# First mixture of a three-stage kernel: second product in whole float32 from an unsplit w2, and the low parts of w1 all on VectorE

## The chip, the cores and the metric

The program runs on one core of a Trainium2 chip. TensorE (PE in the profile) multiplies, VectorE (DVE), ScalarE (ACT) and GpSimd (POOL) do elementwise work, and SyncE (SP) and GpSimd issue the DMAs. The metric is the device time of one execution in microseconds.

## The reference

```
x   = attention(q, k, v)                       # 4 x 8 heads x 576 x 64 -> 2304 tokens of 512
# first mixture: 8 experts, 288 tokens each, given out greedily by logit
logits = x @ w_gate
...
for e in range(8):
    mask = assigned == e                       # 288 tokens
    h = np.maximum(x[mask] @ w1[e], 0.0)       # w1[e]: 512 x 1024
    out[mask] = h @ w2[e]                      # w2[e]: 1024 x 512
# second mixture: two of 8 experts for each token, weighted
logits = x @ w_gate2 + log1p(exp(x @ w_noise)) * noise
...
    out[mask] += top2_w[mask, k, None] * (np.maximum(x[mask] @ w1[e], 0.0) @ w2[e])
```

All tensors are float32.

## The kernel before

There are three stages. Attention fills the first 190 us or so, the first mixture runs from about 220 to 578 us, and the second mixture from there to the end.

In both mixtures a product is made of float32r operands. A float32 array is split in a high part, a rounded copy in float32r (written by ScalarE), and a low part, the array minus the copy (written by VectorE or GpSimd). Each product is three matmuls, in the order of `TERMS`: high by high, high by low, low by high.

An expert n of the first mixture (0 to 7) goes through these steps:

- `route()` finds the tokens of the next expert by counting digits of the logits. A digit is a loop between VectorE and TensorE: VectorE compares (`A`, L624), TensorE counts (`psR`, L633), VectorE tests (`F`, L635), TensorE adds up (L639), VectorE forms the next digit (`vv`, L642). All tiles of this loop but the counts are in SBUF.
- `compact()` makes the token list and gathers the rows of x by three indirect DMAs from GpSimd's queue (`xg`, L728). `xprep1()` transposes them on TensorE (L819) and splits them.
- `weights()` loads w1 and w2 into the four buffers `raw` and splits each in four pieces of 128 x 1024. ScalarE writes the high part (L745); the low part (L747) goes to VectorE or GpSimd by the lists D0 to D4. For experts 0 to 3 VectorE takes two low parts of w1 and GpSimd the other two of w1 and all four of w2. For experts 4 to 7 VectorE takes all four of w1 and two of w2, and GpSimd the other two of w2.
- `gemm_a()` makes the first product (`gemm1`, L835: 8 blocks of 12 matmuls with 288 columns), `relu` writes its result as a high part hh (ScalarE, L847) and a low part hl (VectorE, L848), and the second product (L876) makes 4 blocks of 24 matmuls with 288 columns.
- `rows()` transposes the result, stores it, multiplies it by the gate weights of the second mixture (L910), and `gate2()` works out that mixture's routing in pieces.

`weave` sets the order. Each of these is a generator that yields an estimated time, and the next instructions come from the generator with the smallest clock. Every engine then works through its own list strictly in that order, so a TensorE instruction of the routing that waits for VectorE holds up the products behind it.

Of the kernel before, what the change touches and what calls it, by code (L numbers as in the profile page):

```python
# [536 lines left out]
def moe(ctx, tc, g):  # L537
# [40 lines left out]
    # big buffers  # L578
# [3 lines left out]
    hh = mp.tile([P, KF, SL], F32R, name="hh")  # L582
    hl = mp.tile([P, KF, SL], F32R, name="hl")
    w1 = [[mp.tile([P, FF], F32R, name=f"w1{j}{i}") for i in range(KD)] for j in range(2)]
    w2 = [[mp.tile([P, 2, DM], F32R, name=f"w2{j}{i}") for i in range(KF // 2)] for j in range(2)]
# [8 lines left out]
    # ---- routing of the first mixture  # L594
# [102 lines left out]
    def compact():  # L697
        oh = T["oh"]
        for ph in range(E):
# [3 lines left out]
            # token numbers of the group  # L703
# [30 lines left out]
    # ---- operands of the products, split in two float32r parts  # L734
# [21 lines left out]

    def load2(n, i):
        if n < E:
            src = g["w2a"][bass.ds(REG[n], 1), 2 * i * P:2 * (i + 1) * P, :].rearrange("e (a p) d -> p (e a) d", p=P)
        else:  # L760
            src = g["w2b"][n - E, 2 * i * P:2 * (i + 1) * P, :].rearrange("(a p) d -> p a d", p=P)
        raw_load((2, n, i), src)
# [3 lines left out]
    DV = 4  # L766
    D1 = (1, 3)
    D2 = ()
    D3 = (0, 1, 2, 3)
    D4 = (1, 3)  # L770
    D5 = (3,)
    D6 = (1, 3)
    D0 = (1, 3)

    def on_dve(m, n, i):
        if n >= E:
            return i in (D5, D6)[m - 1]
        if n >= DV:
            return i in (D3, D4)[m - 1]
        return i in (D0 if n == 0 and m == 1 else (D1, D2)[m - 1])  # L780

    def weights():
        for n in range(2 * E):
# [5 lines left out]
            if n < E:  # L789
                yield 6.0  # L790
            yield lambda n=n: emitted["g1"] >= n - 1
            for i in range(KD):
                split((1, n, i), w1[0][i], w1[1][i], on_dve(1, n, i))
                load2(n, i)
                yield 2.4
            emitted["w1"] = n
            yield lambda n=n: emitted["g2"] >= n - 1
            for i in range(KD):
# [28 lines left out]
    HH = (hh, hl)  # L827
# [18 lines left out]
    def relu(pg, f, cols):  # L846
        nc.scalar.activation(hh[:, f, cols], pg, AF.Relu)  # L847
        RELU[0] = nc.vector.scalar_tensor_tensor(hl[:, f, cols], pg, 0.0, hh[:, f, cols].bitcast(F32), op0=OP.max,  # L848
                                                 op1=OP.subtract)

# [4 lines left out]
    def gemm_a():  # L855
        for n in range(E):
# [3 lines left out]
            for f in range(KF):  # L860
                x = gemm1(cols, f)
                if pend:
                    relu(*pend)
# [3 lines left out]
            relu(*pend)  # L867
# [3 lines left out]
            for d in range(KD):  # L871
                pg = ps.tile([P, 512], F32, name="psG", bufs=3)
                k_ = 0
                for f in range(KF):
                    for a, b in TERMS:
                        nc.tensor.matmul(pg[:, :CAP], w2[a][f // 2][:, f % 2, d * P:(d + 1) * P], HH[b][:, f, cols],  # L876
                                         start=k_ == 0, stop=k_ == 3 * KF - 1)
                        k_ += 1
                    if f % 2:
                        yield 6 * CAP / 2400  # L880
# [43 lines left out]
    def slots(a, c0, c1):  # L924
        """source row, row of out and weight of slots, from their digits"""
# [148 lines left out]
    # experts with more than SLOT tokens: a list of the further tiles, worked through at the end  # L1074
# [40 lines left out]
    # ---- the second mixture  # L1115
# [234 lines left out]
```

## Time and profile before

| | us |
|---|---|
| Median of 3 runs | 1051.91 (1051.02 to 1058.09) |
| Profiled execution: first to last instruction (its span, the only time kept of it) | 1046.5 |
| Median less that span | 5.4 |
| First mixture: start of the first product of expert 0 to the last second product | 220 to 578.4 |
| TensorE busy in that stretch | 294.9 of 358.4 |
| GpSimd busy in that stretch | 124.4 |

The profile comes from one execution. Durations are read from it, and a forecast for the runs adds the 5.4 us that lie outside of the span.

### The profile page before, as it was taken

What the parts mean: (1) busy time and instruction counts of PE and PEld (TensorE: products, weight loads), DVE (VectorE), ACT (ScalarE), POOL (GpSimd) and SP (SyncE); (2) the same over time, 40 slices, a digit from 0 to 9 for tenths busy, and PEclk for the clock granted to TensorE, in tenths of its full rate; (3) what the DMA queues carried; (4) which work ended last, traced back from release to release, by engine and by line L of the source; (5) the groups of instructions that cost most, each with busy time, mean ns of one, the idle gap of its engine ahead of it and who ended that gap; (6) DMA issues with size and microseconds to landing.
All of it is one profiled execution on the core that took longest, in us unless ns stands there. A gap on an engine that the chain in (4) does not pass through costs nothing. (4 is left out here: it accounts for less than half of the span.)

```text
span 1046.5 us, 18783 instructions
## 1 busy us (share of the span) xinstructions
PE 935.8 (89%) x6798; PEld 864.0 (83%) x6798; DVE 671.3 (64%) x1804; ACT 402.3 (38%) x807; POOL 556.4 (53%) x636
## 2 busy tenths in 40 slices
PE   7999999558786869969987898999999999999996
PEld 6999999457776869959986877989898988899895
DVE  8776777586777888866776747373747465646521
ACT  6767776043232423442634304422322333333310
POOL 9424332162324241330254768797878888878712
PEclk9999999668887879989998999999999999999999
DMA  9868732055242343444443425253534444442301
GB/s 198 190 136 185 174 97 73 22 185 185 56 147 65 109 145 109 126 135 153 148 160 111 142 71 179 88 178 121 170 125 163 133 144 154 130 165 89 124 27 51
DMA packets 115568, 135.15 MB, mean 129 GB/s; under 512 B 68856, under 2 KB 78072, under 8 KB 115472
## 3 DMA queue, kind: packets, MB, share of 16 engines
q1 hardware_dynamic: 98384, 90.93, 30.4%
q0 software_dynamic: 17088, 42.98, 13.3%
q8 instruction: 55, 0.90, 0.4%
q14 instruction: 41, 0.34, 0.1%
HBM read 110.91 MB, written 24.53 MB: 129 GB/s over the span
## 5 line engine op out<-in xcount | busy, mean ns | idle before, releaser
L835 PE MATMUL psG<-xh,w 128*128 128x312 f32 (+3 forms) x1536 | 351.1, 316 | 12.7 <-DVE y L1265 5.9
L835 PEld LDWEIGHTS psG<-xh,w 128*128 128x128 f32 x1536 | 267.2, 198 | 16.7 <-DVE y L1265 7.4
L747 POOL TENSOR_TENSOR w<-raw,w 128x1024 fp32r<-128x1024 f32 x72 | 181.9, 2549 | 155.2 <-ACT w L745 123.5
L835 PE MATMUL psG<-xl,w 128*128 128x312 f32 (+3 forms) x768 | 241.2, 314 | 0.3 <-DVE tot L1106 0.3
L1233 PE MATMUL psG<-w,hh 128*128 128x512 f32 (+1 forms) x640 | 199.9, 390 | 0.0
L1127 POOL DMA_INDIRECT xrow<-x_dram,sr x160 | 156.7, 980 | 53.6 <-issue 45.3
L848 DVE SCALAR_TENSOR_TENSOR hl<-psG,hh 128x312 fp32r<-128x312 f32 (+3 forms) x192 | 89.5, 470 | 143.4 <-ACT hh L847 143.4
L847 ACT ACTIVATE hh<-psG 128x312 fp32r<-128x312 f32 (+3 forms) x192 | 80.9, 423 | 261.0 <-PE psG L835 259.0
L745 ACT ACTIVATE w<-raw 128x1024 fp32r<-128x1024 f32 x128 | 131.8, 1055 | 62.2 <-PE psG L1233 27.1
L835 PEld LDWEIGHTS psG<-xl,w 128*128 128x128 f32 x768 | 151.9, 198 | 0.9 <-DVE tot L1106 0.5
L1233 PEld LDWEIGHTS psG<-w,hh 128*128 128x128 f32 (+1 forms) x640 | 118.4, 185 | 26.7
L747 DVE TENSOR_TENSOR w<-raw,w 128x1024 fp32r<-128x1024 f32 x56 | 116.8, 2089 | 19.0 <-ACT w L745 18.7
L1233 PE MATMUL psG<-w,hl 128*128 128x512 f32 (+1 forms) x320 | 125.0, 391 | 0.0
L876 PE MATMUL psG<-hh,w 128*128 128x288 f32 x512 | 121.3, 318 | 0.0
L876 PEld LDWEIGHTS psG<-hh,w 128*128 128x128 f32 x512 | 90.8, 202 | 11.4 <-issue 11.2
L876 PE MATMUL psG<-hl,w 128*128 128x288 f32 x256 | 81.0, 316 | 6.6 <-DVE hl L848 6.6
L327 POOL DMA_DIRECT2D xq<-x_dram x60 | 33.0, 556 | 93.8 <-DMA x_dram<-xr 33.0
L728 POOL DMA_INDIRECT xg<-x_dram,ix x24 | 26.0, 1085 | 89.6 <-DVE w L422 72.6
L1267 POOL DMA_INDIRECT out_dram<-y,sx x40 | 43.6, 1089 | 53.3 <-DVE y L1265 45.4
L1233 PEld LDWEIGHTS psG<-w,hl 128*128 128x128 f32 (+1 forms) x320 | 59.3, 185 | 12.7
L1151 ACT ACTIVATE xh<-xt 128x512 fp32r<-128x512 f32 (+1 forms) x40 | 23.1, 617 | 113.4 <-DVE xt L1147 113.4
L253 PE MATMUL pO<-v,pt 128*128 128x65 f32 x448 | 58.9, 269 | 0.2
(282 smaller groups left out, 1460.5 us busy)
## 6 DMA issues: line engine op xcount, KB each, us to landing
raw<-in_moe_w_dram SPq DMA_DIRECT2D x128, 512.0 KB, 3.9
x_dram<-xr SPq DMA_DIRECT2D x18, 264.0 KB, 2.1
out_dram<-zero POOLq DMA_DIRECT2D x18, 256.0 KB, 3.5
x_dram<-x2r SPq DMA_DIRECT2D x96, 48.0 KB, 2.4
rawk<-in_k_dram SPq DMA_DIRECT2D x16, 256.0 KB
rawq<-in_q_dram SPq DMA_DIRECT2D x16, 256.0 KB, 4.5
v<-in_v_dram SPq DMA_DIRECT2D x16, 256.0 KB, 5.3
xq<-x_dram POOLq DMA_DIRECT2D x60, 64.0 KB, 3.5
```

Source lines behind the costliest of these rows:

```text
L253: nc.tensor.matmul(o[:, hh + s, :], pt[:, s, j, :], (vp, vc)[j][:, 2 * hp + s, :], start=j == js[0], stop=j == 1)
L327: (nc.gpsimd if XQP else nc.sync).dma_start(xq[32 * a:32 * (a + 1)], x_dram[c * P:(c + 1) * P, a * P:(a + 1) * P].rearrange("(u t) c -> t ...
L728: nc.gpsimd.indirect_dma_start(out=xg[t], out_offset=None, in_=x_dram[:, :], in_offset=bass.IndirectOffsetOnAxis(ap=ix[:, t:t + 1], axis=0))
L745: nc.scalar.activation(h, t, AF.Copy)
L747: eng.tensor_tensor(l, t, h.bitcast(F32), op=OP.subtract)
L835: nc.tensor.matmul(pg[:, :n], w1[a][kd][:, f * P:(f + 1) * P], XX[b][:, kd, cols], start=k_ == 0, stop=k_ == 3 * KD - 1)
L847: nc.scalar.activation(hh[:, f, cols], pg, AF.Relu)
L848: RELU[0] = nc.vector.scalar_tensor_tensor(hl[:, f, cols], pg, 0.0, hh[:, f, cols].bitcast(F32), op0=OP.max, op1=OP.subtract)
L876: nc.tensor.matmul(pg[:, :CAP], w2[a][f // 2][:, f % 2, d * P:(d + 1) * P], HH[b][:, f, cols], start=k_ == 0, stop=k_ == 3 * KF - 1)
L1127: nc.gpsimd.indirect_dma_start(out=t[:, u * P:(u + 1) * P], out_offset=None, in_=src, in_offset=bass.IndirectOffsetOnAxis(ap=SRC[e, j][u], ...
L1233: nc.tensor.matmul(py[:m], HH[b][:, f, j * P:j * P + m], w2[a][f // 2][:, f % 2, :], start=k_ == 0, stop=k_ == 3 * KF - 1)
L1267: x = nc.gpsimd.indirect_dma_start(out=out[:, :], out_offset=bass.IndirectOffsetOnAxis(ap=IDX[e, j][:n], axis=0), in_=y, in_offset=None, b ...
```

## The change

For the first mixture only:

- w2 is loaded whole, as float32, straight into the tiles that hold the split parts of w2 in the second mixture (`w2f`, two sets of four, one for even and one for odd experts). It is no longer split: 32 high parts on ScalarE and 32 low parts go.
- The first product's result is written once, as float32 (`hf`, two buffers, one for even and one for odd experts), by ScalarE. The 64 low parts hl on VectorE go.
- The second product is one matmul in whole float32 where it was three in float32r: 32 for an expert instead of 96.
- All four low parts of w1 are on VectorE for every expert. The number of these pieces on VectorE stays at 32 in the first mixture, and on GpSimd goes from 32 to none.
- The load of w2 for expert n is issued as soon as the second product of expert n - 2 stands in the program, in one row behind the load of w1. Before, each of its four pieces stood behind a split of w1.
- `weave` is told 8 x 288 / 2400 us instead of 6 x 288 / 2400 us for two matmul groups of the second product.

```diff
+    hf = [mp.tile([P, KF, SL], F32, tag=f"h{j}", name=f"hf{j}", bufs=1)[:, :, :CAP] for j in range(2)]
...
     def load2(n, i):
         if n < E:
             src = g["w2a"][bass.ds(REG[n], 1), 2 * i * P:2 * (i + 1) * P, :].rearrange("e (a p) d -> p (e a) d", p=P)
-        else:
-            src = g["w2b"][n - E, 2 * i * P:2 * (i + 1) * P, :].rearrange("(a p) d -> p a d", p=P)
+            t = W2F[n, i] = mp.tile([P, 2, DM], F32, tag=f"w2{n % 2}{i}", name="w2f", bufs=1)
+            nc.sync.dma_start(t, src)
+            return
+        src = g["w2b"][n - E, 2 * i * P:2 * (i + 1) * P, :].rearrange("(a p) d -> p a d", p=P)
         raw_load((2, n, i), src)
...
     def on_dve(m, n, i):
-        if n >= E:
-            return i in (D5, D6)[m - 1]
-        if n >= DV:
-            return i in (D3, D4)[m - 1]
-        return i in (D0 if n == 0 and m == 1 else (D1, D2)[m - 1])
+        return n < E or i in (D5, D6)[m - 1]
...
             if n < E:
                 yield 6.0
+                yield lambda n=n: emitted["g2"] >= n - 2
+                for i in range(KD):
+                    load2(n, i)
             yield lambda n=n: emitted["g1"] >= n - 1
             for i in range(KD):
                 split((1, n, i), w1[0][i], w1[1][i], on_dve(1, n, i))
-                load2(n, i)
+                if n >= E:
+                    load2(n, i)
                 yield 2.4
             emitted["w1"] = n
+            if n < E:
+                emitted["w2"] = n
+                continue
...
+    def relu_whole(n, pg, f, cols):
+        nc.scalar.activation(hf[n % 2][:, f, :], pg, AF.Relu)
...
                 for f in range(KF):
-                    for a, b in TERMS:
-                        nc.tensor.matmul(pg[:, :CAP], w2[a][f // 2][:, f % 2, d * P:(d + 1) * P], HH[b][:, f, cols],
-                                         start=k_ == 0, stop=k_ == 3 * KF - 1)
-                        k_ += 1
+                    nc.tensor.matmul(pg[:, :CAP], W2F[n, f // 2][:, f % 2, d * P:(d + 1) * P], hf[n % 2][:, f, :],
+                                     start=f == 0, stop=f == KF - 1)
                     if f % 2:
-                        yield 6 * CAP / 2400
+                        yield 8 * CAP / 2400
```

GpSimd's list before, from the gathers of expert 0 to those of expert 2 (`w` are parts of w1 and w2):

```order
L728 DMA xg<-x_dram,ix 96x528 x3
L747 TENSOR_TENSOR w_3095<-raw,w_3091 128x1024
L747 TENSOR_TENSOR w_3097<-raw,w_3093 128x1024
L747 TENSOR_TENSOR w_3103<-raw,w_3099 128x1024
L747 TENSOR_TENSOR w_3104<-raw,w_3100 128x1024
L747 TENSOR_TENSOR w_3105<-raw,w_3101 128x1024
L747 TENSOR_TENSOR w_3106<-raw,w_3102 128x1024
L728 DMA xg<-x_dram,ix 96x528 x3
```

And GpSimd's list now, from there to the first weights of the second mixture (`xrow` are gathers of that mixture):

```order
L1278 MEMSET spacer 1x1 x39
L737 DMA xg<-x_dram,ix 96x528 x24
L1139 DMA xrow<-x_dram,sr_6852 128x128 x12
L756 TENSOR_TENSOR w_3093<-raw,w_3089 128x1024
L756 TENSOR_TENSOR w_3094<-raw,w_3090 128x1024
L756 TENSOR_TENSOR w_3095<-raw,w_3091 128x1024
```

The 24 gathers of the eight experts stand in one row, with no elementwise work between them.

VectorE's list before, where w1 of expert 1 is split while the next expert is routed:

```order
L624 TENSOR_TENSOR A<-vv,jrow 128x9x32
L629 SCALAR_TENSOR_TENSOR u<-vv,dg 128x18
L848 SCALAR_TENSOR_TENSOR hl<-psG,hh 128x288
L747 TENSOR_TENSOR w_3096<-raw,w_3092 128x1024
L635 TENSOR_SCALAR F<-psR 16x8
L642 TENSOR_SCALAR vv<-u,psR 128x18
L624 TENSOR_TENSOR A<-vv,jrow 128x2304
L629 SCALAR_TENSOR_TENSOR u<-vv,dg 128x18
L747 TENSOR_TENSOR w_3098<-raw,w_3094 128x1024
L635 TENSOR_SCALAR F<-psR 128x8
```

And VectorE's list now at the same place (L633, L638, L644, L651 and L756 are L624, L629, L635, L642 and L747 of before):

```order
L633 TENSOR_TENSOR A<-vv,jrow 128x9x32
L638 SCALAR_TENSOR_TENSOR u<-vv,dg 128x18
L756 TENSOR_TENSOR w_3093<-raw,w_3089 128x1024
L644 TENSOR_SCALAR F<-psR 16x8
L756 TENSOR_TENSOR w_3094<-raw,w_3090 128x1024
L651 TENSOR_SCALAR vv<-u,psR 128x18
L633 TENSOR_TENSOR A<-vv,jrow 128x2304
L638 SCALAR_TENSOR_TENSOR u<-vv,dg 128x18
L756 TENSOR_TENSOR w_3095<-raw,w_3091 128x1024
L644 TENSOR_SCALAR F<-psR 128x8
L818 TENSOR_TENSOR xl<-psT,xh 128x288 x2
L651 TENSOR_SCALAR vv<-u,psR 128x18
```

The low part hl is gone from the routing loop, and two more low parts of w1 stand in it.

## Rows read from the trace of the kernel before

**Rows 1.** The page, its head and part 1: busy us, share, instructions.

```profile
span 1046.5 us, 18783 instructions
PE 935.8 (89%) x6798; PEld 864.0 (83%) x6798; DVE 671.3 (64%) x1804; ACT 402.3 (38%) x807; POOL 556.4 (53%) x636
```

**Rows 2.** Windows: stretch, length, busy us by engine, granted clock (PEclk), DMA.

```profile
220.00:578.40 358.40, 294.93 (x2545) 281.59 (x2546) 266.40 (x789) 132.16 (x238) 124.41 (x69) 0.87 0.41 126
...
503.80:532.90 29.10, 29.07 (x231) 28.26 (x229) 25.05 (x80) 16.17 (x27) 6.50 (x3) 1.00 0.52 166
...
605.00:1046.50 441.50, 422.39 (x2400) 378.46 (x2398) 227.96 (x269) 126.53 (x212) 322.58 (x284) 1.00 0.38 125
```

**Rows 3.** Waits of TensorE, 215 to 580 us: total, times, longest.

```profile
PE psR L633 <- DVE A L624: 15.8, 3, 8.5
PE psT L819 <- DMA xg<-x_dram,ix: 10.9, 5, 4.4
PE psQ L1010 <- DVE gM L997: 7.6, 1, 7.6
PE psR L676 <- DVE sc L673: 6.9, 1, 6.9
PE psG L876 <- DVE hl L848: 6.6, 3, 2.8
PE psQ L1053 <- DVE gmd L1051: 6.0, 3, 3.6
PE psR L639 <- DVE F L635: 3.4, 1, 3.4
```

**Rows 4.** Timeline, 318 to 335 us, three engines: start, duration, instruction [idle before].

```profile
322.95 9.28 POOL L747 TENSOR_TENSOR w<-raw,w 128x1024 fp32r<-128x1024 f32 x4
...
322.42 9.85 DVE L642 TENSOR_SCALAR vv<-u,psR 128x18 bf16<-128x18 f32 x1 [0.71 <-PE psR L639]
332.30 1.36 DVE L624 TENSOR_TENSOR A<-vv,jrow 128x2304 bf16<-128x2304 bf16 x1
...
333.72 0.64 PE L633 MATMUL psR<-O,A 128*128 128x8 bf16 x18 [8.50 <-DVE A L624]
```

**Rows 5.** Groups of instructions, 190 to 600 us: low parts of weights.

```profile
L747 POOL TENSOR_TENSOR w<-raw,w 128x1024 fp32r<-128x1024 f32 x37 | 94.7, 2582 | 153.3 <-ACT w L745 122.0 <-PE psG L876 30.9 <-PE psG L835 0.3
...
L747 DVE TENSOR_TENSOR w<-raw,w 128x1024 fp32r<-128x1024 f32 x35 | 46.7, 1342 | 1.3 <-ACT w L745 1.0 <-issue 0.2
```

**Rows 6.** Matmuls of attention in whole float32: durations min/median/max in ns; timeline.

```profile
L188 PE MATMUL pS<-kf,qf x64: 275/275/579, 7.0 to 146.5; 128*128 128x128 f32 x64
...
L253 PE MATMUL pO<-v,pt x448: 218/275/325, 15.7 to 181.3; 128*128 128x65 f32 x150
...
94.63 0.61 PE L188 MATMUL pS<-kf,qf 128*128 128x128 f32 x4
```

**Rows 7.** Timeline, second product of expert 0 in float32r.

```profile
262.72 0.29 PE L876 MATMUL psG<-hl,w 128*128 128x288 f32 x1
...
263.51 0.29 PE L876 MATMUL psG<-hl,w 128*128 128x288 f32 x1
```

**Rows 8.** Windows of the 15 stretches at half clock: TensorE, granted clock.

```profile
329.30:343.00 13.70, 9.28 (x70) 0.51 0.25 52
...
sum 92.80, PE 74.49; mean PE 4.97
```

**Rows 9.** Timeline of VectorE, 405 to 416 us: low parts of w1 of expert 4.

```profile
408.61 1.22 DVE L747 TENSOR_TENSOR w<-raw,w 128x1024 fp32r<-128x1024 f32 x1
...
414.42 1.22 DVE L747 TENSOR_TENSOR w<-raw,w 128x1024 fp32r<-128x1024 f32 x1
```

**Rows 10.** Gathers of x: two on GpSimd's timeline, and their landing time.

```profile
319.56 0.91 POOL L728 DMA_INDIRECT xg<-x_dram,ix  x1 [12.41 <-DVE w L422]
...
450.07 2.81 POOL L728 DMA_INDIRECT xg<-x_dram,ix  x1 [0.30 <-issue]
...
DMA to landing us min/median/max: 3.0/4.6/7.5
```

More of the change, by code (lines that the diff above doesn't have):

```diff
@@ L581, in moe, with second_operands, second_weights @@
     xl = mp.tile([P, KD, SL], F32R, name="xl")
-    hh = mp.tile([P, KF, SL], F32R, name="hh")
-    hl = mp.tile([P, KF, SL], F32R, name="hl")
     w1 = [[mp.tile([P, FF], F32R, name=f"w1{j}{i}") for i in range(KD)] for j in range(2)]
-    w2 = [[mp.tile([P, 2, DM], F32R, name=f"w2{j}{i}") for i in range(KF // 2)] for j in range(2)]
+    hf = [mp.tile([P, KF, SL], F32, tag=f"h{j}", name=f"hf{j}", bufs=1)[:, :, :CAP] for j in range(2)]
+    HH, w2 = [], []
+    def second_operands():
+        if not HH:
+            HH.extend(mp.tile([P, KF, SL], F32R, tag=f"h{j}", name=f"h{'hl'[j]}", bufs=1) for j in range(2))
+    def second_weights():
+        if not w2:
+            w2.extend([mp.tile([P, 2, DM], F32R, tag=f"w2{j}{i}", name=f"w2{j}{i}", bufs=1) for i in range(KF // 2)]
+                      for j in range(2))
     def gpart(n):
@@ L755, in load1 @@
         raw_load((1, n, i), src)
+    W2F = {}
     def load2(n, i):
@@ L759, in load2 @@
             src = g["w2a"][bass.ds(REG[n], 1), 2 * i * P:2 * (i + 1) * P, :].rearrange("e (a p) d -> p (e a) d", p=P)
-        else:
-            src = g["w2b"][n - E, 2 * i * P:2 * (i + 1) * P, :].rearrange("(a p) d -> p a d", p=P)
+            t = W2F[n, i] = mp.tile([P, 2, DM], F32, tag=f"w2{n % 2}{i}", name="w2f", bufs=1)
+            nc.sync.dma_start(t, src)
+            return
+        src = g["w2b"][n - E, 2 * i * P:2 * (i + 1) * P, :].rearrange("(a p) d -> p a d", p=P)
         raw_load((2, n, i), src)
     REG = {}
[L766 to L770, printed above, removed]
     D5 = (3,)
     D6 = (1, 3)
-    D0 = (1, 3)
     def on_dve(m, n, i):
-        if n >= E:
-            return i in (D5, D6)[m - 1]
-        if n >= DV:
-            return i in (D3, D4)[m - 1]
-        return i in (D0 if n == 0 and m == 1 else (D1, D2)[m - 1])
+        return n < E or i in (D5, D6)[m - 1]
     def weights():
@@ L793, in weights @@
                 split((1, n, i), w1[0][i], w1[1][i], on_dve(1, n, i))
-                load2(n, i)
+                if n >= E:
+                    load2(n, i)
                 yield 2.4
             emitted["w1"] = n
+            if n < E:
+                emitted["w2"] = n
+                continue
             yield lambda n=n: emitted["g2"] >= n - 1
+            second_weights()
             for i in range(KD):
@@ L826, in moe @@
     XX = (xh, xl)
-    HH = (hh, hl)
     def gemm1(cols, f):
@@ L846, in relu @@
     def relu(pg, f, cols):
+        second_operands()
+        hh, hl = HH
         nc.scalar.activation(hh[:, f, cols], pg, AF.Relu)
@@ L862, in gemm_a @@
                 if pend:
-                    relu(*pend)
+                    relu_whole(n, *pend)
                 pend = x
@@ L866, in gemm_a @@
             emitted["g1"] = n
-            relu(*pend)
+            relu_whole(n, *pend)
             yield lambda n=n: emitted["w2"] >= n
@@ L872, in gemm_a @@
                 pg = ps.tile([P, 512], F32, name="psG", bufs=3)
-                k_ = 0
                 for f in range(KF):
-                    for a, b in TERMS:
-                        nc.tensor.matmul(pg[:, :CAP], w2[a][f // 2][:, f % 2, d * P:(d + 1) * P], HH[b][:, f, cols],
-                                         start=k_ == 0, stop=k_ == 3 * KF - 1)
-                        k_ += 1
+                    nc.tensor.matmul(pg[:, :CAP], W2F[n, f // 2][:, f % 2, d * P:(d + 1) * P], hf[n % 2][:, f, :],
+                                     start=f == 0, stop=f == KF - 1)
                     if f % 2:
-                        yield 6 * CAP / 2400
+                        yield 8 * CAP / 2400
                 if pend:
```

## The prediction

> **What bounds the kernel now.** The page first: TensorE is busy for 89% of the span, far ahead of the others [rows 1]. That is a mean over stages, so I cut the span in windows. In the second mixture TensorE is busy for 422.4 of 441.5 us at a granted clock of 1.00: nothing is to be had there, and the change does not touch it. In the first mixture, 220 to 578.4 us, it is busy for 294.9 of 358.4 us at a mean clock of 0.87 [rows 2]. So 63.5 us are idle there. And 15 stretches, 92.8 us in all with 74.5 us of TensorE work, ran at half clock, its lower level of 1.2 GHz [rows 8]; that work would take half as long at the upper level, so the low clock costs 74.5 / 2 = 37.2 us. The work itself is 294.9 - 37.2 = 257.7 us at full clock. Expert 6 shows what the stage is without waits: 29.1 us, all busy, clock 1.00 [rows 2].
>
> Then the waits of TensorE in that stage, which say who makes it idle [rows 3]. Most are for VectorE, though VectorE is busy for only 266.4 of 358.4 us. The timeline tells why [rows 4]: at 322.42 us a tiny VectorE instruction of the routing, 18 numbers per partition, takes 9.85 us, and it ends when four low parts on GpSimd (9.28 us in a row from 322.95) end. The comparison A follows, and TensorE, whose next instruction counts A, stands idle for 8.50 us. A short VectorE instruction between SBUF tiles does not run while GpSimd runs a low part. The same pattern, VectorE rows of some 2.4 us that end with a GpSimd row, stands ahead of the waits of 6.9, 5.7, 3.6, 3.4 and some shorter ones. The Trainium skill, "SBUF — State Buffer", section "SBUF: two separate sides", calls the port pair that VectorE and GpSimd share an exclusive lock held for a whole instruction; this trace agrees, with 9.85 us beside 9.28.
>
> **The change part by part.**
>
> *Second product, added time.* Each of 8 experts had 96 matmuls; two rows of the same kind six matmuls apart start 0.79 us apart, so one takes 0.132 us [rows 7]; 768 x 0.132 = 101 us. Now there are 256 in whole float32. Attention has such matmuls: its 32 at L188 show as 64 records [rows 6], two for each. How long a record lasts with 288 columns no row shows. L253 with 65 columns takes 218 ns at least and L188 with 128 columns 275, so 57 / 63 = 0.905 ns for a column [rows 6], where a float32r matmul takes 0.132 / 288 = 0.46. So a record streams its columns twice. With two passes of 288 columns and the 12 ns that a float32r matmul has on top of 288 / 2.4 = 120, a record takes 0.252 us, and 512 of them take 129 us: 28 us more than before. Bounds: were a record one pass, it would be 512 x 0.132 = 68 us, 33 less than before; at 0.905 ns for a column plus those 12 it is 0.273 us and 140 us, 39 more. I take +28, since the slope of rows 6 is that of two passes. All of it lies on TensorE's path.
>
> *Low parts off GpSimd.* 32 pieces of 2.58 us leave GpSimd in the first mixture [rows 5]; on VectorE the number stays. With them go the VectorE delays and TensorE's waits for A at L633, sc, gmd and F: 15.8 + 6.9 + 6.0 + 3.4 = 32.1 us [rows 3]. Eight of the 15 half-clock stretches come right after such waits, the one at 329.3 us with 9.3 us busy among them [rows 8]; together they hold 40.3 of the 74.5 us, and cost 20.2. That is -52 if nothing else comes late.
>
> *hl.* 64 VectorE pieces go, and the second product no longer waits for them: -6.6 us [rows 3]. What it waits for now is ScalarE's copy alone.
>
> *w1 on VectorE.* Experts 0 to 3 get two more pieces each, 8 x 1.21 = 9.7 us, inside the routing loop. Expert 4 already had that: its four pieces run from 408.6 to 415.6 us among the digits [rows 9], and TensorE shows no wait between 404 and 430 us. So I price it at 0, with 9.7 as the upper bound. The cover is TensorE's own second product, some 16 us long.
>
> *Loads.* Bytes are the same. On SP's queue the four loads of w2 now stand behind those of w1 and wait for the second product of expert n - 2; the loads of w1 of the next expert and the stores of result rows queue behind them. They are needed one product later, so 0; the bound is one landing wait of 4.4 us [rows 3] at the start, where eight loads and the first gathers meet.
>
> *What comes late next.* The gathers of x. TensorE waited 10.9 us for them directly and 7.6 through gM, whose VectorE list stood behind a copy that needed the gather [rows 3]. A gather takes GpSimd 0.91 us to issue, but 2.81 beside the four low parts on VectorE at 450 us [rows 10], and lands 3.0 to 7.5 us later. Some of the waits that go have covered such landings. Bounds: -18.5 us (the freed GpSimd issues them early enough) and 8 experts x 1.9 = +15. In the order of the program only the gathers for experts 1 and 4 stand just ahead of low parts, so I take +4.
>
> The Trainium skill speaks against the change here: the same section warns that GpSimd cannot write descriptors while VectorE runs an operation in a two-port mode. By that alone all 24 gathers could be hit, 24 x 1.9 = 46 us by the row's price at most, and the gain would be gone; the second rival below is this mechanism, with part of that price.
>
> Sum: 28 - 52.3 - 6.6 + 0 + 0 + 4 = -27 us. Against the profiled execution that gives a span of 1046.5 - 27 = 1019.5; the median of the runs is 5.4 above the span, so **1025 us**.
>
> **The rivals.** *PE-bound throughout.* If every wait goes but some 10 us of gate work at the end, the first mixture takes 257.7 + 28 + 10 = 296 us instead of 358.4: -62, 990 us. For it: expert 6 is without a gap. Against: the gather waits do not hang on GpSimd's low parts. One-pass records would lead as low.
>
> *The waits move.* The routing and the gathers take the place of the removed waits, TensorE idles as before, and only hl and some clock remain: 28 less some 28 is nothing, 1041 to 1060 us. For it: a loop of five digits ties TensorE to VectorE in the first five experts. Against: expert 4's stretch [rows 9].
>
> *Slower: weight loads in the open.* If the loads of the stationary operand in whole float32 are not hidden behind 288 columns, each record grows by up to the spacing of L188's records: (0.61 - 0.275) / 3 = 0.112 us [rows 6], 512 x 0.112 = 57 us in the second product, 1082 us. It turns the result from 27 / 512 = 0.053 us a record on. Against: L188's spacing is already 0.112 for two passes of 128 columns (0.107), so almost nothing is in the open there.
>
> By the Trainium skill, "TensorE: Matmul & The Clock Gate", part 3 (what overlaps and what doesn't), a weight load overlaps a running matmul only where their row groups differ; all matmuls here use all 128 rows, so this rival would hold. The float32r rows disagree: 0.132 us leaves 12 ns beside 120 of streaming [rows 7].
>
> **How the numbers follow.** My forecast, 1008 to 1041 us, gets 0.60; PE-bound, below 1008, 0.18; the waits move, 1041 to 1060, 0.13; weight loads in the open, above 1060, 0.09. A measurement of this kernel tells 1% (10.5 us) from no change. Faster by more than that is below 1041.4: 0.60 + 0.18 = 0.78; within 1% 0.13; slower 0.09. The range 990 to 1047 leaves out the last case (0.09), some half of the third (0.06) and the edge of the second (0.04).
>
> **What the new profile would show.** Whole-float32 records of the second product some 0.25 us apart, 64 for an expert; no GpSimd low part ahead of the second mixture; no VectorE row of the routing much over 1.4 us in the first mixture; TensorE idle there near 30 us instead of 63.5, half-clock stretches near 40 us instead of 92.8; and a second mixture as long as before. I am wrong if records are 0.3 us or more apart, if the VectorE delays stay without GpSimd's low parts, or if TensorE's waits for gathers grow beyond 30 us.

## Result: 1023 us instead of 1053, and the profile after

The changed kernel took 1023.44 us (median of 4 runs, 1020.71 to 1025.26) where the kernel before took 1053.39 us on the same chip (4 runs, 1051.02 to 1058.09). The ratio is 0.971, 95% interval 0.968 to 0.975: 30 us faster, where 28 were forecast against the median of the runs. The profiled execution took 1025.26 us, its span is 1023.4.

The head of the page after, to be held against [rows 1]:

```profile
span 1023.4 us, 18113 instructions
PE 949.9 (93%) x6542; PEld 844.0 (82%) x6542; DVE 604.7 (59%) x1740; ACT 370.6 (36%) x775; POOL 474.6 (46%) x604
```

TensorE is busy for 14 us more in a span that is 23 us shorter. Windows of the changed kernel: the first mixture, from the start of expert 0's first product to the end of the last second product, and the rest (columns: length, busy us of PE, PEld, DVE, ACT and POOL, granted clock, DMA):

```profile
231.80:555.80 324.00, 300.11 (x2314) 254.55 (x2315) 201.46 (x740) 101.38 (x207) 46.69 (x40) 0.94 0.44 137
555.80:1023.40 467.60, 447.03 (x2541) 402.16 (x2539) 246.04 (x341) 134.25 (x227) 341.58 (x303) 0.99 0.38 125
```

The last line of the windows of its 8 stretches at half clock within the first mixture, against [rows 8]:

```profile
sum 37.40, PE 34.37 PEld 27.89 DVE 19.71 ACT 11.28 POOL 5.11; mean PE 4.30 PEld 3.49 DVE 2.46 ACT 1.41 POOL 0.64
```

From these rows the stage is taken apart as in the prediction. The low clock costs half of the TensorE time in such stretches, 34.37 / 2 = 17.2 us; the work at full clock is 300.1 - 17.2 = 282.9; the idle time is 324.0 - 300.1 = 23.9. Before it was 257.7 of work, 37.2 of clock and 63.5 idle in 358.4 us [rows 2, 8]. So 25.2 us of work came, 20.0 us of clock and 39.6 us of idle time went: -34.4 us. The second mixture is as long as before (467.6 us, and 1046.5 - 578.4 = 468.1 [rows 2]).

The longest waits of TensorE that are left in that window (columns as in [rows 3]):

```profile
PE psT L830 <- DMA xg<-x_dram,ix: 8.7, 5, 4.4
PE psQ L1022 <- DVE gM L1009: 4.2, 1, 4.2
PE psR L642 <- DVE A L633: 3.0, 1, 3.0
```

A's wait fell from 15.8 to 3.0 us, those for sc, gmd and F from 16.3 to 0.8; the gathers head the list. In the window of the first mixture before, 220 to 578.4 us, TensorE waited 6.9 us for them:

```profile
PE psT L819 <- DMA xg<-x_dram,ix: 6.9, 4, 4.4
```

The 10.9 us of [rows 3] count from 215 us on, and 4.0 us of them end at 217.77 us, ahead of the stage.

The rows of vv in the routing, before and after (ns, min/median/max, then the first and the last start in us):

```profile
L642 DVE TENSOR_SCALAR vv<-u,psR x28: 231/245/9845, 196.3 to 421.7; 128x18 bf16<-128x18 f32 x28
```

```profile
L651 DVE TENSOR_SCALAR vv<-u,psR x28: 226/243/245, 205.0 to 394.9; 128x18 bf16<-128x18 f32 x28
```

No row of vv is held up any more. At the end of the stage the old pattern is still there once: the second mixture's first low parts on GpSimd stand beside two small VectorE rows that lead to gM, and the 4.2 us that TensorE waits for gM follow them.

```profile
529.57 4.76 POOL L756 TENSOR_TENSOR w<-raw,w 128x1024 fp32r<-128x1024 f32 x2 [2.52 <-ACT w L754]
```

```profile
530.01 1.99 DVE L987 TENSOR_TENSOR ga<-ga,gw 96x24 f32<-96x24 f32 x1
532.03 2.34 DVE L988 SCALAR_TENSOR_TENSOR ga<-glog,ga 96x24 f32<-96x24 f32 x1
534.40 0.18 DVE L989 TENSOR_TENSOR ga<-ga,gv 96x24 f32<-96x24 f32 x1
```

The span is shorter by 23.1 us only, because attention ended later in this execution. The choice of expert 0 (`ei`, its first start is the first time in the row), of the kernel before and of the changed one:

```profile
L664 DVE TENSOR_SCALAR ei<-em x8: 134/134/135, 206.8 to 431.7; 1x1 int32<-1x1 f32 x8
```

```profile
L673 DVE TENSOR_SCALAR ei<-em x8: 134/134/135, 215.5 to 402.9; 1x1 int32<-1x1 f32 x8
```

The code up to there is the same, and in the profiles of the experiments this choice comes anywhere from 208 to 221 us; those 8.7 us are not the change's. From there to the end it is 1046.5 - 206.8 = 839.7 us before and 1023.4 - 215.5 = 807.9 after, 31.8 less, which agrees with the 30 us that were timed. The terms: 34.4 less in the first mixture, 0.5 less in the second, and 3.1 more between the choice of expert 0 and its first product (16.3 us after, 13.2 before).

### The profile page after: what moved, and what is told of

It reads as the page before. It is cut to its first block, busy times and chain, and to the rows that moved or that the text cites. A ratio compares the mean times of both kernels' runs of the same rounds, so it can differ in the third digit from the quotient of the medians.

```text
span 1023.4 us, 18113 instructions
## 1 busy us (share of the span) xinstructions
PE 949.9 (93%) x6542; PEld 844.0 (82%) x6542; DVE 604.7 (59%) x1740; ACT 370.6 (36%) x775; POOL 474.6 (46%) x604
## 3 DMA queue, kind: packets, MB, share of 16 engines
q0 software_dynamic: 17088, 42.98, 13.5%
## 5 line engine op out<-in xcount | busy, mean ns | idle before, releaser
L845 PE MATMUL psG<-xh,w 128*128 128x312 f32 (+3 forms) x1536 | 340.5, 309 | 12.8 <-DVE hl L860 3.7
L845 PEld LDWEIGHTS psG<-xh,w 128*128 128x128 f32 x1536 | 259.3, 192 | 17.4 <-DVE hl L860 4.4
L889 PE MATMUL psG<-hf,w2f 128*128 128x288 f32 x512 | 149.0, 434 | 1.1 <-ACT hf L864 1.1
L860 DVE SCALAR_TENSOR_TENSOR hl<-psG,hh 128x312 fp32r<-128x312 f32 (+2 forms) x128 | 60.7, 481 | 132.4 <-ACT hh L859 132.3
L756 DVE TENSOR_TENSOR w<-raw,w 128x1024 fp32r<-128x1024 f32 x56 | 103.7, 1865 | 31.9 <-ACT w L754 29.0
L754 ACT ACTIVATE w<-raw 128x1024 fp32r<-128x1024 f32 x96 | 98.3, 1054 | 54.1 <-PE psG L1245 23.8
L889 PEld LDWEIGHTS psG<-hf,w2f 128*128 128x128 f32 x512 | 96.0, 200 | 23.7 <-ACT hf L864 1.3
L859 ACT ACTIVATE hh<-psG 128x312 fp32r<-128x312 f32 (+2 forms) x128 | 55.1, 431 | 155.3 <-PE psG L845 155.3
L756 POOL TENSOR_TENSOR w<-raw,w 128x1024 fp32r<-128x1024 f32 x40 | 98.3, 2474 | 16.5 <-ACT x2t L894 8.7
L1279 POOL DMA_INDIRECT out_dram<-y,sx x40 | 43.9, 1099 | 55.9 <-DVE y L1277 48.1
L1164 DVE TENSOR_TENSOR xl<-xt,xh 128x512 fp32r<-128x512 f32 (+1 forms) x40 | 63.2, 1610 | 9.8 <-ACT xh L1163 9.8
L1163 ACT ACTIVATE xh<-xt 128x512 fp32r<-128x512 f32 (+1 forms) x40 | 23.1, 616 | 119.8 <-DVE xt L1159 119.8
```

The costliest lines, as they stand in the source:

```text
L754: nc.scalar.activation(h, t, AF.Copy)
L756: eng.tensor_tensor(l, t, h.bitcast(F32), op=OP.subtract)
L845: nc.tensor.matmul(pg[:, :n], w1[a][kd][:, f * P:(f + 1) * P], XX[b][:, kd, cols], start=k_ == 0, stop=k_ == 3 * KD - 1)
L889: nc.tensor.matmul(pg[:, :CAP], W2F[n, f // 2][:, f % 2, d * P:(d + 1) * P], hf[n % 2][:, f, :], start=f == 0, stop=f == KF - 1)
L1164: nc.vector.tensor_tensor(xl[:, :, cols], raw[:, :, :n], xh[:, :, cols].bitcast(F32), op=OP.subtract)
L1279: x = nc.gpsimd.indirect_dma_start(out=out[:, :], out_offset=bass.IndirectOffsetOnAxis(ap=IDX[e, j][:n], axis=0), in_=y, in_offset=None, b ...
```

## Experiments

All are edits of the changed kernel, but for the second, an edit of the kernel before, and the tenth, the changed kernel itself. They ran on three further chips, each beside runs of the kernel before: e1 to e4 on one (kernel before 1051.25 us), e5 to e8 on another (1196.47), e9 to e12 on a third (1194.75). On the last two the second mixture took over 100 us longer in every trace of a kernel that routes as the reference does (the kernel before was only timed there), so there I compare ratios, and the first mixture in the traces. Of these chips the changed kernel itself ran on the last alone (e10). On the chip of e1 to e4, e4 can stand for it: its TensorE instructions stand in the same order, and its stage took the same 324.0 us. That e10 took 332.3 us shows how far the stage of one kernel moves from chip to chip or run to run. The table takes that stage apart for each as above, in us, from one profiled execution each.

| kernel | first mixture | work | half clock | idle | VectorE busy | GpSimd busy | ratio to before, 95% interval |
|---|---|---|---|---|---|---|---|
| before | 358.4 | 257.7 | 37.2 | 63.5 | 266.4 | 124.4 | 1 |
| changed | 324.0 | 282.9 | 17.2 | 23.9 | 201.5 | 46.7 | 0.971 (0.968 to 0.975) |
| e1 idle GpSimd work | 341.6 | 285.5 | 18.7 | 37.4 | 235.2 | 133.4 | 0.994 (0.991 to 0.997) |
| e2 before, all lows on VectorE | 337.8 | 259.0 | 32.8 | 46.0 | 247.1 | 46.9 | 0.986 (0.982 to 0.991) |
| e3 w1 lows on GpSimd | 341.5 | 282.1 | 18.4 | 41.1 | 213.3 | 113.6 | 0.989 (0.986 to 0.992) |
| e4 w2 after the gathers | 324.0 | 282.5 | 20.5 | 21.1 | 202.3 | 43.9 | 0.973 (0.966 to 0.980) |
| e5 idle hl | 332.8 | 284.3 | 17.2 | 31.2 | 221.5 | 46.1 | 0.970 (0.967 to 0.973) |
| e6 idle w2 lows | 327.1 | 283.7 | 14.1 | 29.3 | 235.2 | 44.9 | 0.958 (0.955 to 0.960) |
| e7 short second product | 313.7 | 263.6 | 20.9 | 29.2 | 191.0 | 41.1 | - |
| e8 later transposes | 317.4 | 281.7 | 15.6 | 20.1 | 201.7 | 44.6 | 0.951 (0.948 to 0.954) |
| e9 both idle works | 369.0 | 282.2 | 33.1 | 53.7 | 258.7 | 47.0 | 0.989 (0.987 to 0.992) |
| e10 changed again | 332.3 | 283.9 | 21.9 | 26.5 | 201.3 | 45.9 | 0.965 (0.962 to 0.968) |
| e11 relu on VectorE | 331.3 | 283.9 | 19.7 | 27.7 | 219.7 | 45.2 | 0.964 (0.962 to 0.967) |
| e12 later transposes | 316.0 | 283.3 | 14.1 | 18.6 | 201.4 | 45.9 | 0.949 (0.946 to 0.952) |

**e1, idle work on GpSimd.** In `weights()`, behind each split of w1 in the first mixture:

```
+ if n < E:
+     for c in range(2):
+         x = w1[0][i][:, c * DM:(c + 1) * DM].bitcast(F32)
+         nc.gpsimd.tensor_tensor(SCR, x, x, op=OP.subtract)
```

> The changed kernel with GpSimd given back its work, but no duty: behind each split of w1 in the first mixture GpSimd subtracts two halves of the high part from themselves into a scratch tile that nobody reads (64 instructions of 128x512, added work that is no part of the output; about the 82 us of GpSimd time that the low parts took before). Theory (VectorE is held up while GpSimd runs on SBUF tiles): VectorE rows of several us return in the routing, TensorE waits longer for A, and the time is 20 to 45 us above the changed kernel's 1023 us, 1043 to 1068. Rival (TensorE waited for the results of GpSimd's low parts, or the gain is that of hl and the loads): nobody waits for the scratch tile, so 1023 +- 5 us.

It took 1045.78 us. TensorE's and VectorE's instructions stand in the same order as in the changed kernel, and nobody reads the scratch tile; still the stage is 17.6 us longer, 13.5 of it idle time, and VectorE is busy for 235.2 us instead of 201.5 with the same instructions. The profiled execution, at 1033.16 us, was the fastest of the ten, so the usual cost is rather higher. Window of the first mixture, the last line of its stretches at half clock, and the first waits of TensorE in the window:

```profile
226.20:567.80 341.60, 304.21 (x2313) 254.53 (x2314) 235.19 (x740) 101.81 (x207) 133.39 (x98) 0.94 0.42 129
...
sum 40.50, PE 37.46 PEld 28.68 DVE 28.53 ACT 12.39 POOL 18.23; mean PE 4.16 PEld 3.19 DVE 3.17 ACT 1.38 POOL 2.03
```

```profile
PE psT L835 <- DMA xg<-x_dram,ix: 9.2, 4, 4.2
PE psR L642 <- DVE A L633: 5.6, 4, 2.4
PE psT L835 <- DVE xl L823: 5.4, 2, 4.7
```

The wait for A is 2.6 us longer, the one for xl, another VectorE instruction, is new, and the one for the gathers is 0.5 us longer; so it is not that the gathers queue behind GpSimd's idle work. VectorE's routing rows are longer. The timeline of VectorE and GpSimd at 296 us:

```profile
296.86 1.23 DVE L756 TENSOR_TENSOR w<-raw,w 128x1024 fp32r<-128x1024 f32 x1 [0.46 <-ACT w L754]
296.98 4.07 POOL L804 TENSOR_TENSOR scr<-w 128x512 fp32r<-128x512 f32 x2 [15.98 <-ACT w L754]
298.01 1.02 DVE L651 TENSOR_SCALAR vv<-u,psR 128x18 bf16<-128x18 f32 x1
298.93 1.21 DVE L756 TENSOR_TENSOR w<-raw,w 128x1024 fp32r<-128x1024 f32 x1
```

The two engines take turns: two pieces that take 1.04 us each at the shortest last 4.07, and the 18 numbers of vv take 1.02 us instead of 0.24. The time is as the theory has it, near the low end of its range; its rows of several us did not come. Of the rows of vv none lasts over 1.04 us here, where [rows 4] showed 9.85 beside four pieces of 128x1024 in a row. The pieces differ in more than their size: these all write one tile and start some 0.08 us after the one before has ended, while those of [rows 4] follow without a gap (the second starts at 325.31, the first lasts to 325.34). The first two of each kernel:

```profile
296.98 2.01 POOL L804 TENSOR_TENSOR scr<-w 128x512 fp32r<-128x512 f32 x1 [15.98 <-ACT w L754]
299.07 1.98 POOL L804 TENSOR_TENSOR scr<-w 128x512 fp32r<-128x512 f32 x1
```

```profile
322.95 2.39 POOL L747 TENSOR_TENSOR w<-raw,w 128x1024 fp32r<-128x1024 f32 x1
325.31 2.33 POOL L747 TENSOR_TENSOR w<-raw,w 128x1024 fp32r<-128x1024 f32 x1
```

Whether the gap or the size lets VectorE in was not tried.

**e2, all low parts on VectorE in the kernel before.** In `on_dve`:

```
- if n >= DV:
-     return i in (D3, D4)[m - 1]
- return i in (D0 if n == 0 and m == 1 else (D1, D2)[m - 1])
+ return True
```

> The kernel before with one part of the change alone: all low parts of the first mixture, of w1 and of w2, on VectorE; the second product stays in three float32r products and hl stays. Theory (GpSimd's work is what costs; whole float32 is a price of 22 to 28 us on TensorE that saves VectorE 32 x 1.22 = 39 us of low parts and hl): faster than before by 25 us or more, 1005 to 1030 us, and the second product's matmuls stay at 0.13 us. Rival (the gain comes from the whole float32 product, by what it takes off VectorE): VectorE, with 32 x 1.22 = 39 us more than before, becomes the wait, and the time is 1050 us or more.

It took 1033.55 us, 17.7 less than the kernel before, so neither theory's number. The held rows of vv are gone; the group of L642, with up to 9845 ns in the kernel before, is now:

```profile
L642 DVE TENSOR_SCALAR vv<-u,psR x28: 233/243/251, 197.6 to 414.1; 128x18 bf16<-128x18 f32 x28
```

Window of the first mixture, and the last line of its stretches at half clock:

```profile
222.80:560.60 337.80, 291.79 (x2561) 275.87 (x2562) 247.06 (x824) 134.04 (x238) 46.86 (x38) 0.88 0.44 131
...
sum 82.30, PE 65.65 PEld 59.14 DVE 50.92 ACT 24.33 POOL 10.08; mean PE 6.56 PEld 5.91 DVE 5.09 ACT 2.43 POOL 1.01
```

So 46 us of idle time and 32.8 us of clock loss stay. Taking the work off GpSimd is not enough, and the part that I had charged as a pure cost, the product in whole float32 without hl and without low parts of w2, is worth another 13.8 us of the stage on top (337.8 to 324.0), though it adds 23.9 us of TensorE work.

**e3, w1's low parts on GpSimd.**

```
- return n < E or i in (D5, D6)[m - 1]
+ return n >= E and i in (D5, D6)[m - 1]
```

> The changed kernel with the other half of the change undone and more: all 32 low parts of w1 of the first mixture on GpSimd, none on VectorE; the second product in whole float32 as changed. GpSimd then has as many low parts as before. Theory: the held-up VectorE rows return, and with them some 25 to 40 us, 1045 to 1065 us; the waits of TensorE for A are back above 20 us. Rival (VectorE's load is what counts; it is 39 us lighter here than in the changed kernel): 1010 to 1025 us.

It took 1038.56 us, 15 more than the changed kernel and 6 under the theory's range. Window of the first mixture, and the last line of its stretches at half clock:

```profile
225.30:566.80 341.50, 300.43 (x2294) 253.15 (x2295) 213.29 (x706) 101.81 (x207) 113.55 (x69) 0.93 0.43 130
...
sum 48.00, PE 36.76 PEld 28.13 DVE 33.58 ACT 10.46 POOL 18.49; mean PE 4.59 PEld 3.52 DVE 4.20 ACT 1.31 POOL 2.31
```

The wait for A is back, the first of TensorE's in the window (3.0 us in the changed kernel), and a row of vv lasts up to 7.3 us:

```profile
PE psR L642 <- DVE A L633: 22.2, 5, 8.6
```

```profile
L651 DVE TENSOR_SCALAR vv<-u,psR x28: 229/245/7301, 199.1 to 398.1; 128x18 bf16<-128x18 f32 x28
```

The rival falls: VectorE has some 39 us of low parts less, is yet busy for 12 us more, and the stage is 17.5 us longer.

**e4, w2's loads behind the gathers.** In `load2`, for the first of an expert's four loads:

```
+ if gate: nc.sync.dma_start(GATE, XG[n][NT - 1][:1, :16])
```

> The changed kernel with one small transfer added on SP's queue ahead of an expert's four loads of w2: it reads 64 bytes of that expert's last gathered tile, so that the loads start only when the gathers have landed. The rest stands in the same order. Theory (the loads of w2 share the DMA engines with the first gathers; that is the 5 us by which the changed kernel starts its first product later behind the choice of expert 0): that distance falls from 18.2 to some 14 us, the gathers' median from issue to landing from 6.4 to below 5 us, and the time by 4 to 8 us, 1015 to 1020 us. Rival (the gathers are late for another reason, or the loads of w2 now come too late for the second product): no change, 1023 +- 4 us, or up to 10 us slower with waits of TensorE for w2f.

It took 1022.70 us, no change that can be told. The distance from the choice of expert 0 to its first product is 15.1 us instead of 16.3 (the 18.2 of the expectation count to a later product), and the median landing of the gathers 5.7 instead of 6.4 us. One of expert 0's four loads was issued ahead of the small transfer, so the loads were not wholly out of the way, but with three of four behind the gathers 1.2 of 3.1 us came back. Part of the rest is no load: the third gather of expert 0 takes longer to issue where a low part of w1 runs beside it on VectorE. Its row in the kernel before, with no low part beside it, in the changed kernel and in e4 (in e3, with none beside it either, it takes 0.92 us):

```profile
214.06 0.92 POOL L728 DMA_INDIRECT xg<-x_dram,ix  x1 [0.30 <-issue]
```

```profile
222.73 1.49 POOL L737 DMA_INDIRECT xg<-x_dram,ix  x1 [0.31 <-issue]
```

```profile
217.03 1.73 POOL L737 DMA_INDIRECT xg<-x_dram,ix  x1 [0.30 <-issue]
```

What makes up the remainder is open.

**e5, hl as idle work.** In `relu_whole`:

```
+ nc.vector.scalar_tensor_tensor(SCH, pg, 0.0, hf[n % 2][:, f, :], op0=OP.max, op1=OP.subtract)
```

> The changed kernel with hl's 64 VectorE instructions put back as idle work: each computes the difference of relu and its copy, as before, into a scratch tile that nobody reads (added work, no part of the output), 64 x 0.447 = 28.6 us of VectorE in the first mixture. Theory A (whole float32 pays for its longer product by what it takes off VectorE, which the routing and the gathers' indices wait for): 5 to 15 us slower than the changed kernel, 1028 to 1038 us, with longer waits of TensorE for A, gM and xl. Theory B (VectorE has room; what counts is that TensorE does not wait for hl, and that a longer product covers the waits): 1023 +- 5 us.

The stage took 332.8 us. That is 8.8 more than the changed kernel took on the chip of the result, as theory A wants, but e10 showed later that the changed kernel itself takes 332.3 us on a chip of this kind. The ratios (0.970 and 0.965) leave some 6 us; in the profiled executions they lie in the second mixture, which the edit does not touch (599.2 us from the end of the stage, 592.6 in e10). So hl alone costs little or nothing here.

**e6, low parts of w2 as idle work.** In `weights()`, behind the loads of w2:

```
+ for i in range(KD):
+     for a in range(2):
+         nc.vector.tensor_tensor(SCW, W2F[n, i][:, a, :], W2F[n, i][:, a, :], op=OP.subtract)
+     yield 2.4
```

> The changed kernel with the 32 low parts of w2 put on VectorE as idle work, each in two halves of 128x512 that subtract the loaded w2 from itself into a scratch tile that nobody reads (added work, no part of the output), about 39 us of VectorE in the first mixture, among the digits. Theory A (VectorE's load): 10 to 25 us slower than the changed kernel, 1033 to 1048 us. Theory B (VectorE has room): 1023 +- 5 us.

Not slower either: 327.1 us, and a ratio below that of e10. Its yields also put what follows in `weights()` later in the order, so this number holds a change of order too. Theory A falls for each of the two works by itself.

**e7, the second product at its old price.** The kernel leaves out the product with w2: CST is a constant float32r tile that stands in its place, and hf is float32r. A few short matmuls that still read w2 are not shown:

```
- nc.tensor.matmul(pg[:, :CAP], W2F[n, f // 2][:, f % 2, d * P:(d + 1) * P], hf[n % 2][:, f, :],
-                  start=f == 0, stop=f == KF - 1)
+ for c in range(3):
+     nc.tensor.matmul(pg[:, :CAP], CST, hf[n % 2][:, f, :], start=f + c == 0,
+                      stop=f == KF - 1 and c == 2)
...
```

> The changed kernel with the second product of the first mixture at the price of three float32r products again, but with no low part and no hl: each of its matmuls in whole float32 becomes three float32r matmuls of relu's output with one constant 128x128 tile (the output of the first mixture is then not the product with w2; w2 is still loaded and read by four 8-column matmuls per expert). TensorE has 22 us less work at full clock than in the changed kernel, and VectorE the same. Were TensorE's work what sets the stage: 1023 - 22 = 1001 us or less. If the routing, the gathers and the loads set it (theory B: the longer product only fills time that TensorE would wait): above 1013 us, with 10 to 20 us more idle time of TensorE in the first mixture and more of it at half clock.

The second mixture then routes other numbers and took far longer, so only the first mixture is read: 313.7 us. Its work is 20.3 us less than in e10, which ran on another chip of that kind, and the stage 18.6 us shorter; against the changed kernel on the chip of the result it is 19.3 us of work and 10.3 us of the stage. So half or more of the longer product is a real cost. Idle time grew by 3 to 5 us, not by 10 to 20: theory B, that the product only fills idle time, falls.

**e8, later transposes.**

```
- XY = 3
+ XY = 6
```

> The changed kernel with one number other: the transposes of the gathered x are put later in the order of the work (XY 6 in place of 3), behind more of the product that TensorE has at hand. Theory (TensorE stands in front of transposes whose gathers have not landed, 13.9 us in the first mixture, 4.4 us of it at 258.74 us, while products are ready): the waits for xg fall below 8 us and the time by 4 to 8 us, 1015 to 1019 us. Rival (the gathers bound the stage, since the product of the next expert needs them anyway): 1023 +- 4 us, or slower by a later first product of the next expert.

The stage took 317.4 us; TensorE's waits for gathers in it fell from 8.7 us in the changed kernel to 1.7. The two kernels ran on different chips here; e12 has them on one.

**e9, both idle works.** The edits of e5 and e6 together, with one scratch tile.

> The changed kernel with both idle VectorE works put back, hl's 64 and w2's 64 half low parts (added work that nobody reads), about 68 us, so that VectorE does what it does where the second product stays in three float32r products and all low parts are on VectorE. Alone, the first added 8.8 us to the first mixture and the second 3.1. If VectorE's load explains the 46 us of idle time there were without whole float32: the first mixture takes 340 us or more (idle 37 us or more), about 16 us more than the changed kernel. If the two just add up: 336 us, 12 more. If VectorE has room for the second: 333 us, 9 more.

It took 1183.98 us where e10 took 1153.35 on the same chip: 30.6 us slower by the medians, 28.6 by the ratios, and the stage of the profiled execution 36.7 longer. Windows of the first mixture, and the last line of those of its 9 stretches at half clock:

```profile
224.80:593.80 369.00, 315.26 (x2316) 266.97 (x2317) 258.68 (x867) 102.03 (x207) 46.98 (x40) 0.88 0.39 120
...
sum 92.00, PE 66.17 PEld 57.22 DVE 58.38 ACT 24.23 POOL 5.45; mean PE 7.35 PEld 6.36 DVE 6.49 ACT 2.69 POOL 0.60
```

With GpSimd quiet and the product in whole float32, 72 us of VectorE work whose results nobody reads (64 rows of 0.68 and 64 of 0.45 us) bring back both the idle time (53.7 us) and the half-clock stretches (92.0 us, in the kernel before 92.8 [rows 8]). The first of TensorE's waits in the window:

```profile
PE psT L835 <- DMA xg<-x_dram,ix: 15.6, 8, 3.7
PE psR L642 <- DVE A L633: 8.6, 4, 3.3
PE psR L648 <- DVE F L644: 6.6, 8, 2.5
PE psG L850 <- DVE scw L870: 6.4, 3, 5.9
```

What is late is mostly the routing and the gathers, whose indices come from VectorE. Some 7 of the 53.7 us are waits for the idle work itself: in place of hl it reads a PSUM buffer (psG) that TensorE wants to write again. The two works cost far more together than the sum of each alone (the stages of e5 and e6 took 332.8 and 327.1 us, e10's 332.3). ScalarE, which the change relieved of 31 us (132.2 [rows 2] to 101.4), has 102.0 here, so its lighter load is not what the gain hangs on; no run gives its work back alone.

**e10, the changed kernel again.** No edit.

> The changed kernel itself, as the reference on this chip for the three others. On a chip like that of the result: 1023 +- 4 us. Its first mixture, from the first first product to the last second product, took 324.0 us: 282.9 us of TensorE work at full clock, 17.2 lost to half clock, 23.9 idle. If TensorE's clock and the routing's waits repeat, it is 320 to 328 us; attention's end (the choice of expert 0) may lie anywhere from 206 to 216 us.

The ratio is 0.965, the gain here 41 us. The stage took 332.3 us on this chip, and the second mixture 592.6.

**e11, relu on VectorE.**

```
- nc.scalar.activation(hf[n % 2][:, f, :], pg, AF.Relu)
+ nc.vector.tensor_scalar(hf[n % 2][:, f, :], pg, 0.0, None, op0=OP.max)
```

> The changed kernel with relu of the first mixture on VectorE in place of ScalarE (same result): the second product in whole float32 then waits for a VectorE instruction again, as it did for hl, with less VectorE work than hl (no more than 0.447 us each). Theory (what hl cost is mostly that TensorE and the PSUM buffers wait for VectorE's turn among the digits, not VectorE's time): TensorE waits for hf or for a PSUM buffer behind it, the first mixture takes 8 us or more longer, and more of it is at half clock (loss above 20 us). Rival (it is VectorE's time alone): at most 8.8 us longer with a clock loss near 17 us.

1153.28 us beside 1153.35: nothing. The theory falls; that the second product waits for a VectorE instruction costs nothing by itself while VectorE has room.

**e12, later transposes beside the changed kernel.** The edit of e8.

> The changed kernel with the transposes of gathered x put later (XY 6 in place of 3), now beside the changed kernel on one chip. On another chip its first mixture took 317.4 us against 324.0. If the 3.8 us of idle time and 1.6 us of clock that it saved there come from that place: 4 to 8 us faster than the changed kernel beside it (some 1017 where that has 1023). If they came from the other chip: within 3 us of it.

1134.43 us beside 1153.35, 19 us faster (the intervals of the ratios, 0.946 to 0.952 and 0.962 to 0.968, don't meet), so more than expected. Window of the first mixture and TensorE's wait for the gathers in it, of e10:

```profile
225.50:557.80 332.30, 305.77 (x2315) 258.97 (x2316) 201.29 (x740) 101.84 (x207) 45.90 (x40) 0.92 0.43 133
```

```profile
PE psT L830 <- DMA xg<-x_dram,ix: 7.3, 4, 3.5
```

And of e12:

```profile
224.50:540.50 316.00, 297.44 (x2315) 254.32 (x2316) 201.37 (x740) 101.18 (x207) 45.94 (x40) 0.95 0.46 140
```

```profile
PE psT L830 <- DMA xg<-x_dram,ix: 1.7, 2, 0.9
```

Of the 20.6 us between the two profiled executions 16.3 lie in that stage, half of them (7.9) idle time and half (7.8) clock. On this chip this version is faster than both kernels.

## Why the prediction was right, point by point

**The second product, +28: right, and measured at +25.2.** One stretch of the timeline, 28 records of expert 6's second product in a row:

```profile
462.35 6.95 PE L889 MATMUL psG<-hf,w2f 128*128 128x288 f32 x28
```

Less the last record's 0.41 us (403 to 406 ns is what one record shows) that is (6.95 - 0.41) / 27 = 0.242 us a record. Two passes of 288 columns at 2.4 GHz are 0.240, so 2 ns lie on top where I had put 12. 512 x 0.242 = 124 us, 23 more than the 101 before; the other 2 us of the stage's added work I did not trace. The rival with weight loads in the open (0.3 us or more) is out. e7 shows that about half of it (10.3 of 19.3 us) or nearly all (18.6 of 20.3) lies on the path, by the chip that it is held against; I had put all of it there.

**Low parts off GpSimd, -32.1 idle and -20.2 clock: the mechanism is right, the size of this term alone is not.** The held rows of [rows 4] are gone and come back with GpSimd's work where it is needed (up to 7.3 us, e3), and in shorter form where nobody waits for it (e1); so it is GpSimd at work beside VectorE that costs, and no wait for its results. But e1 (in the fastest of its runs) and e3 put 15 and 18 us of idle time and clock back, not 52, and e2 won 22 (17.5 idle, 4.4 clock). The Trainium skill, "SBUF — State Buffer", section "SBUF: two separate sides", has the shared port pair go whole to whichever instruction starts first. The alternation in e1 agrees with that. That VectorE got no turn between four pieces in [rows 4] is not explained by it, nor that the VectorE row has the earlier start there (322.42 us, GpSimd's first piece 322.95); so the prediction's "this trace agrees" holds for e1 rather than for the row that it named.

**hl, -6.6: too small a view.** I priced the waits of TensorE that name hl, and left out the 64 x 0.447 us that it takes on VectorE. What the changed kernel saves besides the held rows is, for the most part, VectorE's time. Idle time and clock loss together, against VectorE's busy time in the stage (held time counted), on all chips and without e7, e8 and e12, whose second product or order is another: 41 us at 201 (changed), 48 at 201 (e10), 42 at 202 (e4), 47 at 220 (e11), 48 at 222 (e5), 43 at 235 (e6), 56 at 235 (e1), 79 at 247 (e2), 87 at 259 (e9), 101 at 266 (before). e3, with its 7 us rows, is off that line (60 at 213). Up to some 220 us, and 235 in e6, VectorE's load costs nothing here that stands out from the 7 us between e10 and the chip of the result. Put back into the changed kernel, GpSimd's work alone costs 15 to 18 us of idle time and clock, hl and the low parts of w2 on VectorE cost next to nothing each (e5, e6), and 38 together (e9). So the sum of my terms for idle time and clock was near (-32.1 - 20.2 - 6.6 + 4 for the gathers = -54.9, measured -59.6), while the split between GpSimd and VectorE's own work has no single value: it depends on which is taken away first. That picture is drawn from single executions on four chips, and but for e1 and e10 the lists of TensorE or VectorE also differ a little in order, so the single numbers carry some us of that. What in the longer VectorE lists makes the clock fall in e2 and e9 (33 us) and not in e3 (18, with 41 us idle) I did not settle; the total idle time alone does not tell it.

**w1 on VectorE, 0: right in the main.** The changed kernel's VectorE runs as many low parts in the first mixture as before, TensorE's waits name none of them, and e11 shows room for 18 us more. At the start one of them stands beside a gather's issue, 0.6 us (e4).

**Loads, 0 with a bound of 4.4: up to +3.1 us at the start,** within the bound. From issue to landing the gathers took a median of 4.6 us before [rows 10] and 6.4 after. e4 gave back 1.2 us; how much more of the 3.1 is the loads' is open.

**Gathers, +4: +1.8 in the stage** (8.7 after, 6.9 before; 4.0 of the 10.9 that the prediction took stand ahead of it). The wait for gM is 3.4 us shorter (7.6 to 4.2), and what is left of it stands behind the two VectorE rows beside GpSimd's low parts of the second mixture, not behind a gather. The Trainium skill's warning in "SBUF — State Buffer", section "SBUF: two separate sides", on descriptors that GpSimd can't write beside VectorE's two-port work, would have been worth up to 46 us by the prediction's row. The issues of gathers in the changed kernel (ns, min/median/max):

```profile
L737 POOL DMA_INDIRECT xg<-x_dram,ix x24: 916/920/2464, 220.2 to 416.6; - x24
```

The median is that of an undisturbed issue, so few of the 24 were hit, and the cost here stays far below the 46 us. The price was also not the rule's own: the row of 2.81 us stood beside low parts, which are tensor_tensor work, and the same section says that tensor_tensor has no two-port mode.

**From span to median, +5.4: wrong, and hidden by another error.** The time of a run is 1.9 us above its own span. The other 3.5 us of the 5.4 were that the profiled execution before lay below the median of its runs; attention's late end in the one after took their place. That 1025 lies within 2 us of the 1023.4 measured is in part luck: from the choice of expert 0 on the kernel gained 31.8 us where the sum has 27, and 8.8 us came on top (8.7 of attention, 1.9 from span to run, less the 1.8 by which the profiled run lay above the median) where the prediction added 5.4.

**The rivals.** PE-bound would have needed 10 us of idle time in 296; it was 23.9, and 17 of clock. The waits did move in small part, to the gathers (6.9 to 8.7 us), but 59 us of idle time and clock went. e12 shows that some 16 us of what was left in e10 could still go.

## What to carry to other kernels

Where a loop of short instructions ties two engines, count the whole load of the slower one, held rows and work whose results nobody reads alike, and try removals together: each alone can look far smaller than it is. A longer instruction stream on the busy engine can pay for itself when it takes work off the engine that keeps it waiting. After such a change look at the first wait that is left: here one number that moved transposes behind products that were ready brought 19 us more.

## What the runs showed of the hardware that was not expected

- Idle GpSimd work of 128x512 pieces and VectorE took turns piece by piece (4.07 us for two pieces of 1.04), where four 128x1024 pieces without a gap held a VectorE row for 9.85 us [rows 4].
- On two of the chips the second mixture took 589 to 599 us instead of 468 (593 in e10, whose TensorE, VectorE, ScalarE and GpSimd instructions are those of the changed kernel in the same order). ScalarE stood there ahead of its copies of relu for something that the profile can't name ("remote"); of its waits from 560 us on in e10:

```profile
ACT hh L859 <- remote: 126.3, 14, 13.7
```

On the chip of the result the changed kernel has no such wait. What it is stays open.
